# Induced attention and a PReLU layer in one kernel: casting weight loads, seven shared PSUM banks, weight folds ahead, idle matmuls, new planner constants

## The chip, the core and the metric

The kernel runs on one core of one Trainium2 chip. The metric is device time in microseconds (us), the median over several executions. The profiled span of an execution is some 2 us shorter than its device time. All profiles below are of single executions. An execution is called slow when it is over 1.5% above the fastest of the same kernel. In the profiles PE is TensorE (PEld its weight loads), DVE VectorE, ACT ScalarE, POOL GpSimd and SP SyncE. The granted clock is the share of TensorE's full clock that the profile records as allowed, 1.0 or 0.5 in these traces. A bank is one of the kernel's tiles in PSUM, the memory that its matmuls write to.

## The reference, cut to what matters

```python
# x: 4 x 12480 x 128 fp32, inducing: 32 x 128, w_in: 128 x 2048, w_out: 2048 x 128, alpha: 2048
def mab(q, kv):
    a = softmax(q @ kv.T / sqrt(128))
    return a @ kv
h = mab(inducing, x)            # per batch: 32 rows that sum up 12480
y = mab(x, h)                   # every row of x attends to the 32 rows of h
g = y @ w_in
out = (max(g, 0) + alpha * min(g, 0)) @ w_out
```

Since y is a weighted mean of 32 rows, the kernel folds h and both weight matrices into small matrices, once for each batch. It never forms the 2048-wide hidden layer, except in a fallback that this input does not need.

## The kernel before

Each of 4 batches has 9 chunks: 8 of 1536 rows and one of 192. A chunk goes through three stages, and each batch through one fold between the first and the second stage:

- A: load x as bf16 (POOL issues the casting load), flip it (DVE), scores (TensorE, 4 matmuls of 384 columns), exp (ACT), flip (DVE), sum into h (TensorE, 12 small matmuls).
- Fold: 20-odd dependent small steps from h to three small matrices SP, ZB, WB.
- S: second scores against h (TensorE), exp, and an extent for a later check.
- O: hidden (SP and mask matmuls), ReLU, ZB and WB matmuls into three banks, eviction with a scale (DVE, or ACT and then POOL), store of 768 KB.

A planner written in Python decides the order on every engine. It plays the tasks with assumed durations, takes the ready task of lowest deadline, and then emits the instructions in that order. The engines keep it whatever the chip does.

```python
RINGS = dict(xn=10, xt=16, s=3, h=1, o=4, e1=3, e1t=3, g=3, ob=4)   # s, h, o: PSUM banks
DR = "s"                                   # the folds' tiles come from the score banks
SLACK = 1.5                                # two numbers in the choice
BIAS = 0.2                                 # between DVE and ACT for evictions
OB = 0.35                                  # assumed time of the WB matmuls
TA, TS, TB, WL, LEAD = 2.6, 1.2, 3.2, 6, 2
def dl_a(b, i): return 2.0 * i if b == 0 else 18.0 + TA * (NCK * (b - 1) + i)   # stage A
def dl_w(b):    return dl_a(b, NCK) + WL
def dl_s(b, i): return dl_a(b, NCK) + TS if i <= 0 else dl_b(b, i) - LEAD        # stage S, fold
def dl_b(b, i): return dl_w(b) + TB * i                                          # stage O
# ... cut ...
def w_loads(_):                            # fp32, issued by SP as soon as it can
    nc.sync.dma_start(out=al[:], in_=moe_alpha.rearrange("(p k) -> p k", p=P))
    nc.sync.dma_start(out=w_in_f[:], in_=moe_w_in)
# ... w_out_f the same way; POOL then casts both to bf16 (1.9 us each) ...
```

The softmax here doesn't subtract the row's maximum and nothing guards it: scores larger than these inputs give would overflow.

## Time and profile before

| | before |
|---|---|
| device time | 177.68 us median of the first 3 runs (176.9 to 179.26) |
| first x landed / first scores | 10.8 / 13.8 us |
| fold of batch 0, from h copied to first hidden matmul | 28.8 to 46.5 us |
| first store issued | 50.8 us |
| end of the fold of batch 3 | 138.8 us |
| store interval in the tail | 3.1 us |

The page of the kernel before; rows of section 2 are 40 slices of 4.4 us, digits are tenths:

```profile
span 176.2 us, 3680 instructions
PE 134.5 (76%) x1322; PEld 65.4 (37%) x1322; DVE 117.4 (67%) x304; ACT 94.2 (53%) x279; POOL 77.6 (44%) x102
...
PEclk9999999659999969999999999997999995555555
DMA  4999999996899999999998586594398564787660
```

TensorE has most work, DMA is full for half of the span, and the granted clock is half over the last seven slices. The average does not show which of them counts; the stretches do. The timeline of the start (start, duration, engine, line, operation, tiles, count, and in brackets the idle time before it and what ended it):

```profile
1.21 0.41 SPq L832 DMA_DIRECT2D w_in_f<-in_moe_w_in_dram  x1
1.67 0.43 SPq L835 DMA_DIRECT2D w_out_f<-in_moe_w_out_dram  x1
1.30 2.83 POOL L357 DMA_DIRECT2D xn<-in_x_dram  x5 [0.35 <-issue]
10.85 0.98 DVE L364 STREAM_TRANSPOSE xt<-xn 128x768 f32<-128x768 f32 x1 [9.39 <-DMA xn<-in_x_dram]
13.83 1.46 PE L373 MATMUL s<-xt,blkI 128*128 128x384 bf16 x4 [13.83 <-ACT blkI L210]
```

One fp32 weight load leaves ahead of the first x load and one 0.4 us after it. They land at 6.3 and 11.0 us, and DVE waits 9.39 us for the first x. The timeline of batch 0's fold, its first and last links and one POOL cast:

```profile
28.84 0.26 ACT L435 COPY hp<-h 128x128 f32<-128x128 f32 x1
29.43 1.90 POOL L841 CAST w_in_b<-w_in_f 128x2048 bf16<-128x2048 f32 x1
```

```profile
46.47 0.24 PE L733 MATMUL hh<-e,sp 128*32 128x128 bf16 x3
```

Two windows of the tail (columns: window, length, busy time and count of PE, PEld, DVE, ACT, POOL, then granted clock, DMA share, GB/s), and one round of the circle in which it is caught, from the timeline:

```profile
140.00:150.00 10.00, 7.16 (x44) 2.45 (x42) 4.30 (x19) 4.97 (x14) 5.41 (x7) 0.73 0.49 170
150.00:160.00 10.00, 7.59 (x38) 2.00 (x37) 5.04 (x11) 2.84 (x7) 3.70 (x4) 0.50 0.86 310
```

```profile
153.21 1.01 PE L758 MATMUL o<-zb,e 128*128 128x512 bf16 x2 [0.93 <-DVE ob L779]
154.01 0.63 PE L758 MATMUL hh<-zb,e 128*128 128x512 bf16 x1
154.57 0.60 PE L767 MATMUL hh<-wb,g 32*128 32x512 bf16 x1
155.38 0.69 DVE L779 TENSOR_TENSOR ob<-hh,rd 128x512 f32<-128x512 f32 x1 [1.63 <-PE o L767]
156.13 1.01 PE L758 MATMUL o<-zb,e 128*128 128x512 bf16 x2 [0.55 <-DVE ob L779]
```

TensorE writes o, DVE evicts it, and the next ZB matmul waits 0.55 or 0.93 us for the bank. At half clock this takes 6.25 us for two chunks.

### The profile page before, as it was taken

How to read it: one execution, taken by the hardware profiler on the slowest of the kernel's cores; microseconds unless marked ns; L12 is line 12 of the kernel's file. 1: busy time of each engine (PE TensorE's matmuls, PEld its weight loads, DVE VectorE, ACT ScalarE, POOL GpSimd, SP SyncE). 2: the span in 40 equal slices, each digit the busy share in tenths (PEclk: the TensorE clock that was granted, in tenths of full speed). 3: DMA queues.
4: the chain of work that ended last, by engine and by line, in shares of the span. 5: the costliest groups of instructions: out<-in, count | busy, mean ns of one | idle time of the engine just before them, and what ended most of it. 6: DMA issues, size and time to landing. Idle time of an engine off the chain costs nothing.

```text
span 176.2 us, 3680 instructions
## 1 busy us (share of the span) xinstructions
PE 134.5 (76%) x1322; PEld 65.4 (37%) x1322; DVE 117.4 (67%) x304; ACT 94.2 (53%) x279; POOL 77.6 (44%) x102
## 2 busy tenths in 40 slices
PE   0006977699999888799998999978988967786600
PEld 0002433456554354355454555434435431121100
DVE  1059596779998997899799886781677553535300
ACT  2024434658377676547969874774875644222300
POOL 7510245409335423865422577332557446523220
PEclk9999999659999969999999999997999995555555
DMA  4999999996899999999998586594398564787660
GB/s 134 355 245 211 213 209 213 212 212 130 162 208 192 268 310 272 351 336 180 224 291 308 183 308 217 198 352 150 118 340 307 183 208 179 269 314 268 226 202 12
DMA packets 23433, 40.82 MB, mean 232 GB/s; under 512 B 1392, under 2 KB 19056, under 8 KB 23152
## 3 DMA queue, kind: packets, MB, share of 16 engines
q1 hardware_dynamic: 18160, 27.67, 44.1%
q0 software_dynamic: 5056, 12.78, 38.7%
q8 instruction: 12, 0.20, 0.4%
q10 hardware_dynamic: 192, 0.07, 0.2%
q14 instruction: 13, 0.11, 0.2%
HBM read 27.73 MB, written 25.56 MB: 303 GB/s over the span
## 4 chain that ended last, share of the span: by engine, by line
PE 54%; DVE 14%; DMA 14%; ACT 5%; issue 5%; POOL 2%; DVEq 0%; POOLq 0%; ACTq 0%
PE s L519 11%; PE s L373 11%; DMA out_dram<-ob 9%; PE o L758 8%; DMA xn<-in_x_dram 5%; DVE ob L779 5%; PE hh L767 5%; PE hh L758 4%; PE h L400 3%; ACT bh L210 3%; PE f L651 2%; PE hh L733 2%; PE hh L739 2%; POOL ob L795 2%; PE hwp L469 2%
## 5 line engine op out<-in xcount | busy, mean ns | idle before, releaser
L795 POOL TENSOR_TENSOR ob<-ob,rd 128x512 f32<-128x512 f32 (+1 forms) x44 | 44.6, 1027 | 45.4 <-ACT ob L784 38.6
L373 PE MATMUL s<-xt,blkI 128*128 128x384 bf16 (+1 forms) x144 | 30.9, 344 | 15.8 <-ACT blkI L210 13.8
L364 DVE STREAM_TRANSPOSE xt<-xn 128x768 f32<-128x768 f32 (+1 forms) x36 | 30.6, 864 | 9.5 <-DMA xn<-in_x_dram 9.4
L357 POOL DMA_DIRECT2D xn<-in_x_dram x36 | 19.9, 556 | 32.6 <-PE h L400 24.8
L519 PE MATMUL s<-xt,bh 128*128 128x384 bf16 (+1 forms) x144 | 30.3, 339 | 4.2 <-ACT bh L210 2.3
L758 PE MATMUL o<-zb,e 128*128 128x512 bf16 x64 | 23.7, 421 | 7.4 <-DVE ob L779 4.4
L779 DVE TENSOR_TENSOR ob<-hh,rd 128x512 f32<-128x512 f32 (+1 forms) x23 | 15.6, 676 | 17.2 <-PE o L767 11.5
L382 ACT ACTIVATE e<-s 128x384 bf16<-128x384 f32 (+1 forms) x36 | 16.6, 462 | 14.6 <-PE s L373 14.0
L784 ACT COPY ob<-o 128x512 f32<-128x512 f32 x31 | 18.1, 588 | 10.1 <-PE o L767 5.6
L373 PEld LDWEIGHTS <-blkI 128*128 128x128 bf16 (+1 forms) x144 | 13.1, 108 | 26.4 <-ACT blkI L210 13.8
L527 ACT ACTIVATE e<-s 128x384 bf16<-128x384 f32 (+1 forms) x36 | 16.6, 460 | 11.0 <-PE s L519 10.5
L779 DVE TENSOR_TENSOR ob<-o,rd 128x512 f32<-128x512 f32 x33 | 22.2, 677 | 0.0
L519 PEld LDWEIGHTS <-bh 128*128 128x128 bf16 (+1 forms) x144 | 12.8, 105 | 14.3 <-issue 3.5
L753 ACT ACTIVATE g<-hh 96x128 bf16<-96x128 f32 (+1 forms) x36 | 9.5, 266 | 14.8 <-DVE rd L745 12.8
L767 PE MATMUL hh<-wb,g 32*128 32x512 bf16 (+1 forms) x36 | 15.9, 441 | 0.0
L758 PE MATMUL hh<-zb,e 128*128 128x512 bf16 (+1 forms) x36 | 15.6, 433 | 0.1
L390 DVE STREAM_TRANSPOSE e1t<-e 128x192 f32<-128x192 f32 (+1 forms) x36 | 11.9, 343 | 3.9 <-ACT e L382 3.6
L767 PE MATMUL o<-wb,g 32*128 32x512 bf16 x64 | 14.2, 439 | 0.0
L758 PEld LDWEIGHTS <-e 128*128 128x128 bf16 (+1 forms) x100 | 9.4, 101 | 12.7 <-issue 9.1
L745 DVE RECIPROCAL rd<-hh 128x12 f32<-128x12 f32 (+1 forms) x36 | 7.7, 216 | 9.5 <-PE hh L739 9.5
L537 ACT ACTIVATE junk<-s 128x384 bf16<-128x384 f32 (+1 forms) x29 | 13.9, 480 | 0.0
L784 ACT COPY ob<-hh 128x512 f32<-128x512 f32 (+1 forms) x13 | 7.3, 558 | 8.4 <-PE o L767 2.8
(111 smaller groups left out, 168.8 us busy)
## 6 DMA issues: line engine op xcount, KB each, us to landing
out_dram<-ob SPq DMA_DIRECT2D x32, 768.0 KB, 4.0
xn<-in_x_dram POOLq DMA_DIRECT2D x32, 384.0 KB, 10.3
w_in_f<-in_moe_w_in_dram SPq DMA_DIRECT2D x1, 1024.0 KB, 5.1
w_out_f<-in_moe_w_out_dram SPq DMA_DIRECT2D x1, 1024.0 KB, 9.3
out_dram<-ob SPq DMA_DIRECT2D x4, 96.0 KB, 2.5
xn<-in_x_dram POOLq DMA_DIRECT2D x4, 48.0 KB, 9.5
ind<-in_inducing_dram ACTq DMA_DIRECT2D x4, 16.0 KB, 5.0
al<-in_moe_alpha_dram SPq DMA_DIRECT2D x1, 8.0 KB, 1.9
```

What stands on the lines that cost most here:

```text
L357: nc.gpsimd.dma_start(out=v["xn"][: c.p, : c.nk, :], in_=x[s.b, c.t0 : c.t0 + c.n, :].rearrange("(p j) c -> p j c", p=c.p),)
L364: nc.vector.transpose(out=xT[: c.p, : c.nk].rearrange("p k b j e -> p (k b j e)").bitcast(f32), in_=v["xn"][: c.p, : c.nk, :].bitcast(f32),)
L373: nc.tensor.matmul(v["sc"][: c.p, :], blkI[: c.p, bb, e, : c.na, :].rearrange("p a m -> p (a m)"), s.xT[c.i][: c.p, : c.nk, bb, :, e], sta ...
L382: nc.scalar.activation(out=v["e1"][: c.p, : c.w].rearrange("p (K j e) -> p K j e", j=M, e=2), in_=v["sc"][: c.p, :].rearrange("p (K e j) - ...
L519: nc.tensor.matmul(w["sc"][: c.p, :], BH[r][: c.p, bb, e, : c.na, :].rearrange("p a m -> p (a m)"), s.xT[c.i][: c.p, : c.nk, bb, :, e], st ...
L527: nc.scalar.activation(out=s.e2[: c.p, c.off : c.off + c.w].rearrange("p (r j k) -> p r j k", j=M, k=c.nkk), in_=w["sc"][: c.p, :].rearran ...
L537: nc.scalar.activation(out=junk[: c.p, : c.w], in_=w["sc"][: c.p, :], func=SQUARE, accum_out=amx[: c.p, 0, b, c.i : c.i + 1],)
L758: nc.tensor.matmul(o[: c.po, :], s.e2[: c.p, c.off + q * c.po : c.off + (q + 1) * c.po], ZB[r][: c.p].rearrange("p a c -> p (a c)"), start ...
L767: nc.tensor.matmul(v["o", q][: c.po, :], v["g"][rows, : c.po], WB[r][rows].rearrange("p a c -> p (a c)"), start=False, stop=True,)
L779: nc.vector.tensor_tensor(out=ob[: c.po, : c.na, q, :], in0=o[: c.po, : c.na, :], in1=bc(rd, [[1, c.na], [0, C]]), op=ALU.mult,)
L784: nc.scalar.copy(out=ob[: c.po, : c.na, q, :], in_=o[: c.po, : c.na, :])
L795: nc.gpsimd.tensor_tensor(out=ob, in0=ob, in1=bc(s.rd[: c.po, c.i, q, : c.na], [[1, c.na], [0, C]]), op=ALU.mult,)
```

## The change

Its intent: get the weights out of the way of the first x and save the casts on POOL; let any stage use any of seven PSUM banks, so that outputs can hold six; let the folds, on which all outputs of a batch wait, go first; keep TensorE's clock up with idle matmuls where the planner sees a pause. With it came new planner constants and four more buffers for flipped x (the room of the fp32 weights).

```diff
-RINGS = dict(xn=10, xt=16, s=3, h=1, o=4, e1=3, e1t=3, g=3, ob=4)
-DR = "s"
+RINGS = dict(xn=10, xt=20, p=7, h=1, e1=3, e1t=3, g=3, ob=4)
+CAPS = dict(A=3, S=3, F=7, O=6)          # stage A scores, stage S scores, folds, outputs
-SLACK = 1.5
-BIAS = 0.2
+SLACK = 3.0
+FILL = 0.5
+BIAS = 0.1
@@ Plan.play
+                if eng == "PE":
+                    self.fill(now, free.get(eng, 0.0))
+    def fill(self, now, end):
+        n = int(FILL * (now - end) / 0.22)
+        ok = [i for i, f in enumerate(self.free["p"]) if f is not None and f <= end]
+        if n > 0 and ok:                  # n matmuls of 512 columns on blkI, into a free bank
+            i = min(ok, key=lambda i: self.free["p"][i])
+            self.order.append(("PE", dict(fn=lambda _: self.filler(n), held={"p": (i, "")}, ...)))
@@ ... tasks take "p:A", "p:S", "p:F", "p:O" in place of "s" and "o" ...
-    OB = 0.35
-    TA, TS, TB, WL, LEAD = 2.6, 1.2, 3.2, 6, 2
+    PW = 16.5
+    FB = 100.0
+    OB = 0.42
+    TA, TS, TB, WL, LEAD = 2.2, 1.2, 3.5, 14, 1
@@ fold_batch
-        prio = dl_s(b, -1)
+        prio = dl_s(b, -1) - FB           # also for the first second scores and the later links
@@ weights
-        nc.sync.dma_start(out=w_in_f[:], in_=moe_w_in)
+        nc.gpsimd.dma_start(out=w_in_b[:], in_=moe_w_in)      # casts on the way, prio PW: after batch 0's x
@@ ... w_out the same; the two POOL casts are gone; the rest of the diff is cut ...
```

More of the change, by code (lines that the diff above doesn't have):

```diff
@@ L63, in __init__ @@
         self.tasks = []
-        self.rings = {k: dict(n=n, taken=0, back=[]) for k, n in RINGS.items()}
+        self.free = {k: [0.0] * n for k, n in RINGS.items()}
+        self.used = {}
+        self.now = None
+        self.before = None
     def add(self, eng, fn, deps=(), take=(), give=(), prio=0, bytes=0):
@@ L79, in play @@
         todo = list(self.tasks)
-        order = []
+        self.order = order = []
         while todo:
@@ L110, in play @@
                 for k in t["take"]:
-                    r = self.rings[k]
-                    i = r["taken"] - r["n"]
-                    if i >= 0:
-                        if r["back"][i] is None:
-                            blocked = True
-                            break
-                        at = max(at, r["back"][i] + self.HOP)
+                    k, c = (k + ":").split(":")[:2]
+                    f = min((f for f in self.free[k] if f is not None), default=None)
+                    if f is None or (c and self.used.get(c, 0) >= CAPS[c]):
+                        blocked = True
+                        break
+                    at = max(at, f + (self.HOP if f else 0.0))
                 if blocked:
@@ L134, in play @@
                 for k in t["take"]:
-                    r = self.rings[k]
-                    t["held"][k] = r["taken"]
-                    r["taken"] += 1
-                    r["back"].append(None)
+                    k, c = (k + ":").split(":")[:2]
+                    f = self.free[k]
+                    i = min((i for i in range(len(f)) if f[i] is not None), key=lambda i: f[i])
+                    f[i] = None
+                    t["held"][k] = (i, c)
+                    self.used[c] = self.used.get(c, 0) + 1
                 for k, owner in t["give"]:
-                    self.rings[k]["back"][owner["held"][k]] = end
+                    i, c = owner["held"][k]
+                    self.free[k][i] = end
+                    self.used[c] -= 1
                 todo.remove(t)
@@ L148, in play @@
         self.total = max(t["end"] for t in self.tasks)
-        self.order = order
+    def fill(self, now, end):
[3 more added lines that the diff above has]
+            i = min(ok, key=lambda i: self.free["p"][i])
+            self.order.append(("PE", dict(fn=lambda _: self.filler(n), held={"p": (i, "")}, start=end, end=end+n*.22, prio=0, eng={"PE":n*.22})))
     def emit(self):
         for eng, t in self.order:
+            self.now = t
             t["fn"](eng)
+        self.now = None
 @with_exitstack
@@ L196, with filler, make_slots, ring @@
     PS = bass.MemoryType.PSUM
-    pools = {}
-    for k, n in ((k, n) for k, n in RINGS.items() if n):
-        space = dict(space=PS) if k in ("s", "d", "h", "o") else {}
-        pools[k] = ctx.enter_context(tc.tile_pool(name="r_" + k, bufs=n, **space))
-    def ring(k, shape, dtype, name=None):
-        return pools[k].tile(shape, dtype, tag=k, name=name or k)
+    def filler(n):
+        p = ring("p")
+        for _ in range(n):
+            nc.tensor.matmul(
+                p[:], blkI[:, 0, 0].rearrange("p a m -> p (a m)"), blkI[:].rearrange("p b e a m -> p (b e a m)"),
+                start=True, stop=True,
+            )
+    plan = Plan()
+    plan.filler = filler
+    add = plan.add
+    slots, turn = {}, {}
+    def make_slots(shapes):
+        for k, (shape, dtype) in shapes.items():
+            pool = ctx.enter_context(
+                tc.tile_pool(name="r_" + k, bufs=1, **(dict(space=PS) if k in ("p", "h") else {}))
+            )
+            slots[k] = [pool.tile(shape, dtype, name=f"{k}{i}") for i in range(RINGS[k])]
+            turn[k] = 0
+    def ring(k, shape=None):
+        if plan.now:
+            i = plan.now["held"][k][0]
+        else:
+            i = turn[k]
+            turn[k] = (i + 1) % RINGS[k]
+            if k == "p":
+                turn[k] = max(2, turn[k])
+        t = slots[k][i]
+        if shape is None:
+            return t
+        n = math.prod(shape[1:])
+        t = t[: shape[0], :n]
+        return t if len(shape) == 2 else t.rearrange("p (a b) -> p a b", b=shape[2])
     def on(eng):
@@ L239 @@
     al = const.tile([P, KC], f32, name="al")
-    w_in_f = const.tile([C, DFF], f32, name="w_in_f")
-    w_out_f = const.tile([P, KC, C], f32, name="w_out_f")
     w_in_b = const.tile([C, DFF], bf16, name="w_in_b")
@@ L293, in small_act @@
             nc.scalar.copy(out=selq[rows, q], in_=sel4[rows])
+    make_slots(dict(
+        xn=([P, NK, C], bf16), xt=([P, NK, 2, M, 2], bf16), p=([P, 512], f32), h=([P, C], f32),
+        e1=([P, NK * M], bf16), e1t=([P, NK // 2, M, 2], bf16), g=([P, P], bf16),
+        ob=([P, G, NK // 4, C], f32),
+    ))
     flags = keep.tile([1, B + 1], i32, name="flags")
@@ L330, in dl_b @@
         return dl_w(b) + TB * i
-    plan = Plan()
-    add = plan.add
     def dve(n, fast=1):
@@ L343, in pool_batch @@
         s = bt[b]
-        s.xT, s.pr = [], []
+        s.xT = {}
         s.h = None
@@ L355, in load @@
         def load(_):
-            v["xn"] = ring("xn", [P, NK, C], bf16)
+            v["xn"] = ring("xn")
             nc.gpsimd.dma_start(
@@ L362, in flip @@
         def flip(_):
-            xT = ring("xt", [P, NK, 2, M, 2], bf16)
+            xT = ring("xt")
             nc.vector.transpose(
@@ L367, in flip @@
             )
-            s.xT.append(xT)
+            s.xT[c.i] = xT
         def scores(_):
-            v["sc"] = ring("s", [P, c.w], f32)
+            v["sc"] = ring("p", [P, c.w])
             for n, (bb, e) in enumerate(((0, 0), (0, 1), (1, 0), (1, 1))):
@@ L380, in exps @@
         def exps(_):
-            v["e1"] = ring("e1", [P, NK * M], bf16)
+            v["e1"] = ring("e1")
             nc.scalar.activation(
@@ L388, in flip_e @@
         def flip_e(_):
-            v["e1t"] = ring("e1t", [P, NK // 2, M, 2], bf16)
+            v["e1t"] = ring("e1t")
             nc.vector.transpose(
@@ L396, in sums @@
             if c.i == 0:
-                s.h = ring("h", [P, C], f32)
+                s.h = ring("h")
             for k in range(c.nk):
@@ L411, in pool_chunk @@
         s.flips.append(tf)
-        ts = add(("PE", 0.05 + 4 * c.w / 2400), scores, [tf], take=["s"], prio=prio)
-        te = add(("ACT", 0.23 + act(c.w)[1]), exps, [ts], take=["e1"], give=[("s", ts)], prio=prio)
+        ts = add(("PE", 0.05 + 4 * c.w / 2400), scores, [tf], take=["p:A"], prio=prio)
+        te = add(("ACT", 0.23 + act(c.w)[1]), exps, [ts], take=["e1"], give=[("p", ts)], prio=prio)
         tt = add(dve(c.w // 2), flip_e, [te], take=["e1t"], give=[("e1", te)], prio=prio)
@@ L431, in dtile @@
         def dtile(shape, name):
-            return ring(DR, shape, f32, name)
+            return ring("p", shape)
         def f_hp(_):
@@ L495, in fold_batch @@
         t = add(act(C), f_hp, [s.pooled], give=[("h", s.first_sum)], prio=prio)
-        t = t_tot = add(("PE", 0.35), f_tot, [t, small], take=[DR], prio=prio)
-        t_n = add(("DVE", 0.5), f_norm, [t], give=[(DR, t_tot)], prio=prio)
+        t = t_tot = add(("PE", 0.35), f_tot, [t, small], take=["p:F"], prio=prio)
+        t_n = add(("DVE", 0.5), f_norm, [t], give=[("p", t_tot)], prio=prio)
         t = add(("DVE", 0.22), f_flip, [t_n], prio=prio)
         t_b = [
-            add({"DVE": 0.28, "ACT": 0.3}, lambda e, a=a: blocks(a, e, BH[r], v["h4t"]), [t], prio=prio)
+            add({"DVE": 0.28, "ACT": 0.3}, lambda e, a=a: blocks(a, e, BH[r], v["h4t"]), [t] + s.free_h, prio=prio)
             for a in range(G)
         ]
-        t = t_hT = add(("PE", 0.15), f_hT, [t_n], take=[DR], prio=prio)
-        t = add(act(M), f_hTc, [t], give=[(DR, t_hT)], prio=prio)
-        t = t_hwp = add(("PE", 1.0), f_hwp, [t, w_in_done], take=[DR], prio=prio)
-        t_hw = add(act(KC * M), f_hw, [t], give=[(DR, t_hwp)], prio=prio)
+        t = t_hT = add(("PE", 0.15), f_hT, [t_n], take=["p:F"], prio=prio)
+        t = add(act(M), f_hTc, [t], give=[("p", t_hT)], prio=prio)
+        t = t_hwp = add(("PE", 1.0), f_hwp, [t, w_in_done], take=["p:F"], prio=prio)
+        t_hw = add(act(KC * M), f_hw, [t], give=[("p", t_hwp)], prio=prio)
         t = add(dve(KC * M), f_hs, [t_hw], prio=prio + 0.1)
@@ L516, in scores @@
             def scores(_):
-                w["sc"] = ring("s", [P, c.w], f32)
+                w["sc"] = ring("p", [P, c.w])
                 for n, (bb, e) in enumerate(((0, 0), (0, 1), (1, 0), (1, 1))):
@@ L547, in second @@
             ts = add(
-                ("PE", 0.05 + 4 * c.w / 2400), scores, t_b, take=["s"],
+                ("PE", 0.05 + 4 * c.w / 2400), scores, t_b, take=["p:S"],
                 give=[("xt", s.flips[c.i])], prio=pr,
@@ L554, in second @@
                 del either["DVE"]
-            tx = add(either, extent, [ts, te], give=[("s", ts)], prio=pr)
+            tx = add(either, extent, [ts, te], give=[("p", ts)], prio=pr)
+            s.scored.append(ts)
             return tx, te
-        s.extents, s.weighed = [], []
+        s.extents, s.weighed, s.scored = [], [], []
         for c in chunks:
-            tx, tq = second(c, dl_s(b, c.i))
+            tx, tq = second(c, dl_s(b, c.i) - (0.0 if c.i else FB))
             s.extents.append(tx)
             s.weighed.append(tq)
-        prio = dl_s(b, 0)
+        prio = dl_s(b, 0) - FB
         def g_ext(_):
@@ L690, in fold_batch @@
         t = add(("ACT", 0.3), g_ext, s.extents[:1], prio=prio)
-        t = t_dlp = add(("PE", 0.2), g_dlp, [t], take=[DR], prio=prio)
-        t = add(dve(M), g_dm, [t], give=[(DR, t_dlp)], prio=prio)
+        t = t_dlp = add(("PE", 0.2), g_dlp, [t], take=["p:F"], prio=prio)
+        t = add(dve(M), g_dm, [t], give=[("p", t_dlp)], prio=prio)
         t_st = add(("DVE", 0.7), g_st, [t, t_sg], prio=prio)
-        t = t_pos = add(("PE", 0.3), g_base, [t_st], take=[DR], prio=prio)
+        t = t_pos = add(("PE", 0.3), g_base, [t_st], take=["p:F"], prio=prio)
         t_sl = add(("DVE", 0.34), g_sl, [t_st], prio=prio)
@@ L697, in fold_batch @@
         t_p0 = add(dve(KC * CAP), g_pick, [t_pos], prio=prio)
-        t_fl = add(("DVE", 0.16), g_flag, [t_pos, t_p0], give=[(DR, t_pos)], prio=prio)
+        t_fl = s.flagged = add(("DVE", 0.16), g_flag, [t_pos, t_p0], give=[("p", t_pos)], prio=prio)
         t_om = add(("POOL", 1.05), g_om, [t_p0, t_sl], prio=prio)
-        t = t_fs = add(("PE", 1.0), g_fs, [t_p0], take=[DR], prio=prio)
-        t_s = add({"ACT": 0.22, "DVE": 0.18}, g_fzs, [t], give=[(DR, t_fs)], prio=prio)
-        t = t_f = add(("PE", 1.2), g_f, [t_om, t_p1, wo_done], take=[DR], prio=prio)
-        t = add({"ACT": 0.29, "DVE": 0.28}, g_fz, [t, t_s], give=[(DR, t_f)], prio=prio)
-        t = t_r = add(("PE", 0.3), g_rep, [t], take=[DR], prio=prio)
-        t = f1 = add(("DVE", 0.2), g_sp, [t, s.free_r], prio=prio)
-        f2 = add(dve(G * C), lambda _: g_blk(0, ZB[r], mask), [t, s.free_r], prio=prio)
-        f3 = add(dve(G * C), lambda _: g_blk(1, WB[r], afmask), [t, f2, s.free_r],
-                 give=[(DR, t_r)], prio=prio)
+        t = t_fs = add(("PE", 1.0), g_fs, [t_p0], take=["p:F"], prio=prio)
+        t_s = add({"ACT": 0.22, "DVE": 0.18}, g_fzs, [t], give=[("p", t_fs)], prio=prio)
+        t = t_f = add(("PE", 1.2), g_f, [t_om, t_p1, wo_done], take=["p:F"], prio=prio)
+        t = add({"ACT": 0.29, "DVE": 0.28}, g_fz, [t, t_s], give=[("p", t_f)], prio=prio)
+        t = t_r = add(("PE", 0.3), g_rep, [t], take=["p:F"], prio=prio)
+        t = f1 = add(("DVE", 0.2), g_sp, [t] + s.free_r, prio=prio)
+        f2 = add(dve(G * C), lambda _: g_blk(0, ZB[r], mask), [t] + s.free_r, prio=prio)
+        f3 = add(dve(G * C), lambda _: g_blk(1, WB[r], afmask), [t, f2] + s.free_r,
+                 give=[("p", t_r)], prio=prio)
         s.folded = [f1, f2, f3]
@@ L721, in emit_batch, with one @@
         r = b % 2
-        def one(c):
+        def one(c, before):
             prio = dl_b(b, c.i)
@@ L729, in hidden @@
             def hidden(_):
-                v["hh"] = hh = ring("o", [P, 512], f32, "hh")
+                v["hh"] = hh = ring("p")
                 for q in range(c.nq):
@@ L750, in relu @@
             def relu(_):
-                v["g"] = ring("g", [P, P], bf16)
+                v["g"] = ring("g")
                 rows = slice(0, c.nq * M)
@@ L755, in outs_a @@
             def outs_a(q):
-                v["o", q] = o = v["hh"] if q == 0 else ring("o", [P, G * C], f32)
+                v["o", q] = o = v["hh"] if q == 0 else ring("p")
                 nc.tensor.matmul(
@@ L773, in move @@
                 if q == 0:
-                    v["ob"] = ring("ob", [P, G, NK // 4, C], f32)
+                    v["ob"] = ring("ob")
                 rd = s.rd[: c.po, c.i, q, : c.na]
@@ L800, in one @@
             th = add(
-                ("PE", 0.15 + 0.02 * c.nq), hidden, [s.weighed[c.i]] + s.folded, take=["o"], prio=prio,
+                ("PE", 0.2 + 0.02 * c.nq), hidden, [s.weighed[c.i], before] + s.folded, take=["p:O"], prio=prio,
             )
@@ L807, in one @@
             for q in range(1, c.nq):
-                tos.append(add(("PE", 0.22), lambda _, q=q: outs_a(q), [th], take=["o"], prio=prio))
+                tos.append(add(("PE", 0.22), lambda _, q=q: outs_a(q), [th], take=["p:O"], prio=prio))
             to = add(("PE", 0.22), lambda _: outs_a(0), [tr, ti] + tos, prio=prio)
@@ L813, in one @@
                     {"DVE": 0.675, "ACT": 0.57, "ACT4": 1.5}, lambda e, q=q: move(e, q),
-                    [t_ob] + moves[:1], take=["ob"] if q == 0 else [], give=[("o", tos[q])], prio=prio,
+                    [t_ob] + moves[:1], take=["ob"] if q == 0 else [], give=[("p", tos[q])], prio=prio,
                 )
@@ L823, in one, with al_load, w_in_load @@
             add(("NONE", 0.0), lambda _: None, [td], give=[("ob", moves[0])], prio=prio)
-            return th, t_ob
-        last = [one(c) for c in chunks][-1]
-        s.emitted = last
-    def w_loads(_):
+            return th, t_ob, tos[-1]
+        s.formed = []
+        for c in chunks:
+            s.emitted = one(c, plan.before)
+            s.formed.append(s.emitted[1])
+            plan.before = s.emitted[2]
+    def al_load(_):
         nc.sync.dma_start(out=al[:], in_=moe_alpha.rearrange("(p k) -> p k", p=P))
-        nc.sync.dma_start(out=w_in_f[:], in_=moe_w_in)
+    def w_in_load(_):
+        nc.gpsimd.dma_start(out=w_in_b[:], in_=moe_w_in)
     def w_out_load(_):
-        nc.sync.dma_start(out=w_out_f[:], in_=moe_w_out.rearrange("(p k) c -> p k c", p=P))
+        nc.gpsimd.dma_start(out=WO[:], in_=moe_w_out.rearrange("(p k) c -> p k c", p=P))
     def weights():
-        tw = add(("SP", 0.2), w_loads, [bt[0].loads[2]], prio=17, bytes=2 ** 20)
-        tw2 = add(("SP", 0.1), w_out_load, [bt[0].loads[5]], prio=17.5, bytes=2 ** 20)
-        w_in_done = add(
-            ("POOL", 1.95), lambda _: nc.gpsimd.tensor_copy(out=w_in_b[:], in_=w_in_f[:]), [tw], prio=18
-        )
+        ta = add(("SP", 0.1), al_load, prio=0, bytes=2 ** 13)
+        w_in_done = add(("POOL", 0.6), w_in_load, prio=PW, bytes=2 ** 20)
+        wo_done = add(("POOL", 0.6), w_out_load, prio=PW + 0.1, bytes=2 ** 20)
         om_done = add(
@@ L847, in weights @@
             ),
-            [tw], prio=18.1,
+            [ta], prio=18.1,
         )
-        t = add(
-            ("POOL", 1.95), lambda _: nc.gpsimd.tensor_copy(out=WO[:], in_=w_out_f[:]), [tw2], prio=24
-        )
-        wo_done = t
         return w_in_done, om_done, wo_done
@@ L867 @@
         s.first_sum = next(t for t in plan.tasks[n0:] if "h" in t["take"])
-        s.free_r = bt[b - 2].emitted[1] if b >= 2 else None
-        s.free_h = bt[b - 2].emitted[0] if b >= 2 else None
+        s.free_r = bt[b - 2].formed if b >= 2 else []
+        s.free_h = bt[b - 2].scored if b >= 2 else []
         fold_batch(b)
@@ L883, in check @@
         )
-        tp = ring(DR, [P, B, M], f32, "tp")
+        tp = ring("p", [P, B, M])
         nc.tensor.matmul(tp[:], ones_f[:], tops[:], start=True, stop=True)
@@ L896, in check @@
         nc.vector.tensor_copy(out=flags[:], in_=flags_f[:])
-    tck = add(("DVE", 2.5), check, [t for s in bt for t in s.extents], take=[DR], prio=dl_b(B - 1, NCK))
-    add(("NONE", 0.0), lambda _: None, [tck], give=[(DR, tck)], prio=dl_b(B - 1, NCK))
+    tck = add(
+        ("DVE", 2.5), check, [t for s in bt for t in s.extents + [s.flagged]], take=["p:F"], prio=dl_b(B - 1, NCK),
+    )
+    add(("NONE", 0.0), lambda _: None, [tck], give=[("p", tck)], prio=dl_b(B - 1, NCK))
     with tc.manual_schedule():
@@ L911, in factors @@
         nc.vector.tensor_tensor(
-            out=W1[:], in0=w_out_f[:], in1=bc(om[:], [[1, KC], [0, C]]), op=ALU.mult
+            out=W1[:], in0=WO[:], in1=bc(om[:], [[1, KC], [0, C]]), op=ALU.mult
         )
@@ L919, in whole @@
         for j in range(DFF // 512):
-            hp = ring("s", [P, 512], f32, "hkp")
+            hp = ring("p")
             for q in range(G):
@@ L930, in whole @@
         )
-        zp = ring("s", [P, C], f32, "zp")
+        zp = ring("p", [P, C])
         for k in range(KC):
@@ L940, in whole @@
         for c in chunks:
-            ob = ring("ob", [P, G, NK // 4, C], f32, "obw")
+            ob = ring("ob")
             for a in range(c.na):
                 rows = slice(a * M, (a + 1) * M)
-                acc = ring("o", [P, NK // 4, C], f32, "acc")
+                acc = slots["p"][a % 2][:, : NK // 4 * C].rearrange("p (a b) -> p a b", b=C)
                 for q in range(c.nq):
@@ L951, in whole @@
                 for f in range(KC):
-                    ph = ring("s", [P, c.w], f32, "ph")
+                    ph = ring("p", [P, c.w])
                     nc.tensor.matmul(
```

## The prediction

> **What bounds the kernel now.** Four stretches of the 176.2 us have four limits.
>
> 1. Start, 0 to 14 us. The chain of waits opens with 9.53 us of "DMA xn<-in_x_dram". The timeline shows why: both fp32 weight loads (2 MB) are issued at 1.2 and 1.7 us and land at 6.3 and 11.0; the first x lands at 10.8. First matmul: 13.8 us.
> 2. 10 to 42 us. DMA share in the windows view is 1.08 at 212 GB/s (bf16 side): one x chunk every 1.86 us. TensorE pauses.
> 3. Fold of batch 0. From copying h (28.8 us) to the first hidden matmul (46.5) is 17.7 us; the first store is issued at 50.8. Between the links stand scores of other chunks, two POOL weight casts of 1.9 us, and a halved clock (0.66 in the 30 to 40 us window).
> 4. 50 to 140 us: TensorE 80 to 100% busy, DVE mostly 71 to 92% (windows view); DMA is full until 90 us, 0.5 to 0.85 after. Tail, 142 to 165 us: clock 0.55, a repeating circle of ZB matmuls 1.0, WB 0.6, eviction 0.7, bank freed; two chunks take 6.25 us. The four "o" banks and the clock set it, not DMA (0.69).
>
> **Costs.**
> - Weights behind the first x: I expect the first x at about 5.5 us (the quickest load took 4.6), first scores near 8.5. This saves about 5 us of head, as batch 0 is paced by its loads. The DMA work stays: 1 MB of bf16 at 211 GB/s is 5 us, later, against some 6.5 before. The POOL casts (3.8 us) vanish.
> - Folds ahead: the links of one fold, added up from the timeline, are about 12 us against 17.7; I expect first stores 4 us earlier. Later folds are overlapped; little comes of them.
> - Seven shared banks, six for outputs: in the tail a second chunk can start while the first is evicted. With the clock held, 1.0 and 0.6 become 0.6 and 0.39. Then 768 KB at about 360 GB/s (moved bytes over busy share) sets 2.15 us per chunk against 3.1: 6 to 7 us over seven chunks.
> - Idle matmuls: they hold the clock in the tail and at 32 to 38 us; two 3.4 us cold spells in the middle vanish. The Trainium skill, "TensorE: Matmul & The Clock Gate", Part 1, says a window of about 3.4 us without enough work halves the clock; this trace agrees (o<-wb matmuls 0.39 us warm, 0.60 after 144.6 us). Cost: they run in order, so real work arriving earlier than planned waits. I subtract 2 us.
> - The middle stays bound by TensorE and DVE (117 us busy): perhaps 2 us gained.
>
> **Floors** (estimates from these rates): x 61 + weights 5 + stores 71 = 137 us of DMA; TensorE about 111 us if warm and dense.
>
> Sum: 176 - 5 - 4 - 6.5 - 2 + 2 = about 161 profiled; on the clock of the runs **162 us, 80% range 154 to 171**. Faster by over 2%: 0.93; within 2%: 0.05; slower: 0.02.
>
> **Right if** the first x lands by 6 us; the first store is issued near 41 us; the granted clock stays near 1.0 to the end; the tail takes under 2.5 us per chunk at DMA share 0.9; DVE share rises to 72% or more.
>
> **Wrong if** fillers delay real matmuls in the full middle; the fold still takes 17 us; shared banks bind stages together; the weights delay batch 0's fold (they must land by 24 us).

## The result, and the profile after

| | before | after |
|---|---|---|
| device time, same rounds | 178.38 us median of 4 | 168.06 us median of 4 (167.86 to 172.95, the last one slow) |
| first x landed / first scores | 10.8 / 13.8 us | 6.1 / 13.7 us |
| fold of batch 0 | 28.8 to 46.5 us | 26.4 to 44.3 us |
| first store issued | 50.8 us | 50.3 us |
| end of the fold of batch 3 | 138.8 us | 127.4 us |
| last store issued | 168.4 us | 159.1 us |
| mean store interval, 27th to 35th | 3.0 us | 2.1 us |

The ratio is 0.9425, with a 95% interval of 0.9333 to 0.9517. A ratio is the mean time of one kernel's fast runs over that of the other's of the same rounds, so not quite the ratio of the medians quoted. The page after:

```profile
span 166.1 us, 3746 instructions
PE 134.3 (81%) x1344; PEld 67.4 (41%) x1353; DVE 117.6 (71%) x304; ACT 91.6 (55%) x276; POOL 79.0 (48%) x106
...
PEclk9999999699999969999999999995978999999555
DMA  4999999999899999999996698762459699989951
```

TensorE's busy time did not change (134.5 and 134.3 us), although the second has idle matmuls in it. The clock's cold end is shorter, and DMA is full again near the end. The start, from the timeline after:

```profile
6.13 0.98 DVE L413 STREAM_TRANSPOSE xt<-xn 128x768 f32<-128x768 f32 x1 [4.66 <-DMA xn<-in_x_dram]
7.61 1.52 ACT L257 COPY blkI<-ind_t 32x128 bf16<-32x128 bf16 x2 [3.72 <-DVE ind_t L281]
9.19 4.69 PE L218 MATMUL p<-blkI 128*128 128x512 bf16 x11 [9.19 <-ACT blkI L257]
13.71 0.82 PE L422 MATMUL p<-xt,blkI 128*128 128x384 bf16 x4
```

The first x came 4.7 us earlier. But at 9.19 us, when the block matrix blkI was ready and the first scores could have started, 11 idle matmuls started in their place. They read blkI, so they could not start sooner, in the pause for which they were planned. They took 4.69 us at half speed (0.43 us from start to start, against 0.22 for those at 14.4 us), and the scores began at 13.71 us: 0.12 us earlier than before. Batch 0's fold, from the timeline after:

```profile
26.43 0.27 ACT L484 COPY hp<-h 128x128 f32<-128x128 f32 x1 [0.60 <-PE h L449]
```

```profile
31.34 2.72 PE L568 MATMUL p<-xt,bh 128*128 128x384 bf16 x8
32.04 0.32 ACT L617 ACTIVATE dsel<-sel,amx 128x32 f32<-128x32 f32 x1
33.86 0.39 PE L621 MATMUL p<-dsel,ones_f 128*128 128x32 f32 x2
34.75 2.12 PE L568 MATMUL p<-xt,bh 128*128 128x384 bf16 x12
41.37 2.12 PE L422 MATMUL p<-xt,blkI 128*128 128x384 bf16 x12
41.57 0.19 DVE L729 TENSOR_TENSOR sp<-p,mask 128x32 bf16<-128x32 f32 x1
44.26 0.22 PE L783 MATMUL p<-e,sp 128*32 128x128 bf16 x3
```

From h copied to the first hidden matmul it is 17.8 us, against 17.6 (46.47 less 28.84) before. "Ahead" is only the planner's rank: when a link is not yet ready by the plan, other scores go into TensorE's queue, here 8, 12 and 12 matmuls, and the next link stands behind them. The link dsel is written by 32.36 us and its matmul starts at 33.86; SP is written by 41.76 us and the first hidden matmul starts at 44.26. The tail after, in the same windows as before, and some lines of its timeline:

```profile
140.00:150.00 10.00, 9.02 (x72) 3.55 (x69) 6.33 (x15) 5.12 (x16) 5.28 (x6) 1.00 0.92 325
150.00:160.00 10.00, 4.83 (x27) 1.75 (x25) 4.85 (x18) 3.67 (x12) 4.07 (x4) 0.68 0.84 293
```

```profile
142.53 0.81 PE L568 MATMUL p<-xt,bh 128*128 128x384 bf16 x4
145.53 0.82 PE L568 MATMUL p<-xt,bh 128*128 128x384 bf16 x4
149.21 0.83 PE L568 MATMUL p<-xt,bh 128*128 128x384 bf16 x4
150.51 0.36 PE L568 MATMUL p<-xt,bh 96*96 96x64 bf16 x4
153.56 0.80 PE L935 MATMUL p<-tops,ones_f 128*128 128x128 f32 x2 [1.63 <-DVE tops L930]
```

The clock is 1.00 up to 153.5 us, and DMA moves 325 GB/s where it moved 170. No idle matmul holds this clock: all 28 in the trace start between 9.2 and 28 us. What stands between the output chunks is second scores of batch 3 (p<-xt,bh), up to 150.9 us. In the kernel before these ended at 140.1 us, and the clock fell at 144.6:

```profile
139.81 0.33 PE L519 MATMUL s<-xt,bh 96*96 96x64 bf16 x4
```

The stores say where the gain lies. Up to the 26th of 36, issued at 140.5 us before and 138.0 after, the two kernels are within 3 us for most stores, and for some the change is behind. The last ten bring the other 7 us: from the 27th to the 35th the mean interval is 3.0 us before and 2.1 us after.

### The profile page after: what moved, and what is told of

The parts are those of the page before. It is cut to its first block, busy times and chain, and to the rows that moved or that the text cites. A ratio compares the mean times of both kernels' runs of the same rounds, so it can differ in the third digit from the quotient of the medians.

```text
span 166.1 us, 3746 instructions
## 1 busy us (share of the span) xinstructions
PE 134.3 (81%) x1344; PEld 67.4 (41%) x1353; DVE 117.6 (71%) x304; ACT 91.6 (55%) x276; POOL 79.0 (48%) x106
## 5 line engine op out<-in xcount | busy, mean ns | idle before, releaser
L829 DVE TENSOR_TENSOR ob<-p,rd 128x512 f32<-128x512 f32 (+1 forms) x52 | 33.1, 674 | 8.8 <-PE p L817 6.0
L808 PE MATMUL p<-zb,e 128*128 128x512 bf16 (+1 forms) x94 | 33.0, 398 | 3.2 <-ACT g L803 1.5
L834 ACT COPY ob<-p 128x512 f32<-128x512 f32 (+1 forms) x48 | 26.0, 582 | 10.5 <-PE p L817 7.1
L568 PE MATMUL p<-xt,bh 128*128 128x384 bf16 (+1 forms) x144 | 27.9, 330 | 3.4 <-DVE bh L259 1.6
L422 PE MATMUL p<-xt,blkI 128*128 128x384 bf16 (+1 forms) x144 | 27.2, 312 | 0.1
L431 ACT ACTIVATE e<-p 128x384 bf16<-128x384 f32 (+1 forms) x36 | 16.7, 464 | 17.1 <-PE p L422 16.6
L576 ACT ACTIVATE e<-p 128x384 bf16<-128x384 f32 (+1 forms) x36 | 16.6, 464 | 13.7 <-PE p L568 13.5
L218 PE MATMUL p<-blkI 128*128 128x512 bf16 x28 | 10.0, 473 | 9.5 <-ACT blkI L257 9.2
L422 PEld LDWEIGHTS <-blkI 128*128 128x128 bf16 (+1 forms) x144 | 12.7, 102 | 10.0 <-issue 1.7
L817 PE MATMUL p<-wb,g 32*128 32x512 bf16 (+1 forms) x100 | 15.0, 407 | 0.1
L449 PE MATMUL h<-xn,e1t 128*32 128x128 bf16 x392 | 11.8, 228 | 0.8 <-DVE e1t L439 0.6
L586 ACT ACTIVATE junk<-p 128x384 bf16<-128x384 f32 (+1 forms) x26 | 12.2, 469 | 0.0
```

The lines of the kernel that those rows point to most:

```text
L422: nc.tensor.matmul(v["sc"][: c.p, :], blkI[: c.p, bb, e, : c.na, :].rearrange("p a m -> p (a m)"), s.xT[c.i][: c.p, : c.nk, bb, :, e], sta ...
L431: nc.scalar.activation(out=v["e1"][: c.p, : c.w].rearrange("p (K j e) -> p K j e", j=M, e=2), in_=v["sc"][: c.p, :].rearrange("p (K e j) - ...
L449: nc.tensor.matmul(s.h[q * M : (q + 1) * M, :], v["e1t"][: c.p, k // 2, :, k % 2], v["xn"][: c.p, k, :], start=(c.i == 0 and k < G), stop= ...
L568: nc.tensor.matmul(w["sc"][: c.p, :], BH[r][: c.p, bb, e, : c.na, :].rearrange("p a m -> p (a m)"), s.xT[c.i][: c.p, : c.nk, bb, :, e], st ...
L576: nc.scalar.activation(out=s.e2[: c.p, c.off : c.off + c.w].rearrange("p (r j k) -> p r j k", j=M, k=c.nkk), in_=w["sc"][: c.p, :].rearran ...
L808: nc.tensor.matmul(o[: c.po, :], s.e2[: c.p, c.off + q * c.po : c.off + (q + 1) * c.po], ZB[r][: c.p].rearrange("p a c -> p (a c)"), start ...
```

## The experiments

Twelve kernels ran besides the change, all with right results. The medians are of all runs of a kernel, slow ones too (three of four in a_nofill and a_xt16, three of six in n1, two of five in b_weights, one of four in the change, a_fb0 and b_fold); the ratios are of fast runs, against the kernel before of the same rounds. In "order kept" runs no engine's order of other work differs from the kernel they are made from; idle matmuls do not enter the planner's times, so taking them away keeps the order. Where a planner input was changed the whole order shifts, and luck of a few us is possible.

| run | median us | ratio (95%) | what |
|---|---|---|---|
| the change | 168.06 | 0.9425 (0.9333 to 0.9517) | |
| a_nofill | 167.26 | none (one fast run, 163.51) | no idle matmuls; order kept |
| a_nolead | 164.49 | 0.9226 (0.9163 to 0.9289) | first burst of idle matmuls gone; order kept |
| a_split | 170.36 | 0.9551 (0.9480 to 0.9622) | banks 3 + 4 |
| a_split_nofill | 170.98 | 0.9552 (0.9464 to 0.9640) | the same, no idle matmuls; order kept |
| a_fb0 | 175.82 | 0.9838 (0.9753 to 0.9924) | folds not ahead |
| a_oldc | 173.26 | 0.9697 (0.9625 to 0.9769) | old constants |
| a_xt16 | 172.56 | none (one fast run, 167.96) | 16 flipped-x buffers |
| b_weights | 183.92 | 1.0280 (1.0206 to 1.0354) | before + the weights' part |
| b_w_order | 179.49 | 1.0048 (0.9973 to 1.0123) | the same, order kept |
| b_fold | 191.17 | 1.0644 (1.0535 to 1.0753) | before + folds ahead |
| n1 | 166.99 | 0.9273 (0.9183 to 0.9363) | a_nolead + 4 constants |
| n2 | 170.04 | 0.9498 (0.9410 to 0.9587) | n1 + folds ahead by 2 only |

### The idle matmuls

```diff
 a_nofill, from the change:
-FILL = 0.5
+FILL = 0.0
 a_nolead, from the change:
-        n = int(FILL * (now - end) / 0.22)
+        n = int(FILL * (now - end) / 0.22) if end else 0     # none before the first real matmul
```

Expected of a_nofill:

> The changed kernel with no idle matmuls at all; the order of all other instructions stays the same, as fillers do not enter the plan's times. In the changed kernel all 28 traced idle matmuls start between 9.2 and 28 us, 11 of them in one burst of 4.7 us right before the first scores. Theory H (the burst delays the first scores and eats the head's gain; the gain of the whole change comes from the banks in the tail): first scores near 9.2 us instead of 13.7, but cold ones (1.46 us per chunk); time 165 to 169 us. Rival F (the fillers' warm clock is a main source of the gain): 172 us or more.

Expected of a_nolead:

> The changed kernel without the first burst of 11 idle matmuls alone; later ones stay. Theory H: first scores near 9.2 us, fold of batch 0 begins 2 to 4 us earlier than 26.4 us, and up to that much of it reaches the end: 164 to 167 us. If the middle is bound by engines whatever the start, the end moves by less than 1 us: 167 to 168. Rival F (the burst pays by warming the clock): slower than 168.

Measured: a_nolead 164.49 us, the only interval clear below that of the change. Its first scores, from its timeline:

```profile
9.13 1.46 PE L422 MATMUL p<-xt,blkI 128*128 128x384 bf16 x4 [9.13 <-ACT blkI L257]
10.39 1.91 PE L218 MATMUL p<-blkI 128*128 128x512 bf16 x4
```

They start 4.6 us earlier, cold (1.46 us for four where the change has 0.82), and the next four idle matmuls follow them, where DVE has to flip the second chunk. The fold of batch 0 begins at 23.3 us instead of 26.4. Up to the 21st store the lead is 1.6 to 2.0 us; it is 2.8 at the 22nd and 4.9 at the last store but one (the 35th, issued at 152.3 us instead of 157.2). The growth sets in just after a cold spell that the change has at 122.8 us and this trace has not; whether the burst brings that spell about was not tested. So theory H held for the first scores and the time, and the rival that the burst pays by warming the clock fell: the burst costs 3.6 us of medians, of which the head start itself is about half. The other half of theory H, that the gain comes from the banks, is tested next. In a_nofill three of four runs were slow (167.2 to 167.4 us at a granted clock of 0.897) and one was fast (163.51 us at 0.928, below theory H's range). Against fast runs of a_nolead (164.1 to 165.7) the remaining idle matmuls bring nothing; that they make slow runs rarer (0 of 4 against 3 of 4) is suggested by these counts, not shown.

### The banks

```diff
 a_split, from the change (a_split_nofill: also FILL = 0.0):
-CAPS = dict(A=3, S=3, F=7, O=6)
+CAPS = dict(A=3, S=3, F=3, O=4)
-                    if f is None or (c and self.used.get(c, 0) >= CAPS[c]):
+                    if f is None or (c and self.used.get(c, 0) >= CAPS[c]) or (
+                        c and c != "O" and sum(self.used.get(u, 0) for u in "ASF") >= 3):
```

Expected of a_split:

> The changed kernel with the seven banks split as before: at most 3 for scores and folds together, at most 4 for outputs; everything else stays. Theory S (the six output banks make the tail): the last stores come 3 us apart instead of 2, and most of the 10 us is lost: 174 to 179 us. Rival O (order and constants alone bring the last fold 11 us earlier and fill the tail): 167 to 170 us.

Measured: 170.36 us, 2.3 us over the change, with intervals that overlap a little. Theory S fell; O was right to within half a microsecond. With four output banks the stores of the tail come 1.8 us apart (27th to 35th), not 3. Its trace has what the change lacks, 15 idle matmuls after 130 us.

Expected of a_split_nofill:

> The run with the banks split three and four, and no idle matmuls as well. The split run took 170.4 us; its trace has idle matmuls between the output chunks of the tail, and the clock stays at 1.0 there until 159 us, where the kernel before has 0.5 from 144.6 us on. Theory C (with four output banks the idle matmuls keep the clock, and with it the tail's pace): tail at clock 0.5 and near 3 us per chunk as in the kernel before; the 3.6 us of the first burst come back, but the tail loses 6 to 8 us: 172 to 176 us. Rival (the tail's pace is set by order, not by the clock): 166 to 168 us, the 3.6 us of the burst gained and nothing lost.

Measured: 170.98 us. Windows of a_split and then of a_split_nofill:

```profile
140.00:150.00 10.00, 9.52 (x75) 3.35 (x73) 7.76 (x18) 4.49 (x12) 5.17 (x5) 1.00 0.94 333
```

```profile
140.00:150.00 10.00, 9.74 (x49) 2.25 (x47) 5.59 (x13) 3.23 (x9) 3.77 (x4) 0.50 0.87 306
```

Without idle matmuls the clock is 0.50 here (from 132.2 to 152.7 us in all), with them 1.00, and DMA moves 306 against 333 GB/s. At the 25th store a_split_nofill is still 0.9 us ahead (138.8 against 139.7 us), the remainder of what it saved at the start; at the 35th it is 2.6 us behind (160.5 against 157.9). So idle matmuls do what they are for where the planner puts them into a tail: 3.5 us between these two traces. Theory C had the mechanism right and the size too large: 170.98 us lies between the two ranges. Even with a cold clock the stores came 2.6 us apart (22nd to 32nd), not 3.

### The folds' priority

```diff
 a_fb0, from the change:
-    FB = 100.0
+    FB = 0.0
 b_fold, from the kernel before:
-        prio = dl_s(b, -1)
+        prio = dl_s(b, -1) - 100.0
-            tx, tq = second(c, dl_s(b, c.i))
+            tx, tq = second(c, dl_s(b, c.i) - (0.0 if c.i else 100.0))
-        prio = dl_s(b, 0)
+        prio = dl_s(b, 0) - 100.0
```

Expected of a_fb0:

> The changed kernel with the folds at their old priority; all else stays. Theory P (folds ahead bring the last fold's end to 127 us from 139 us and so start the tail early): last fold's end at 132 us or later, 171 to 176 us. Rival (the folds' priority changes little, since each fold waits in TensorE's queue behind scores either way: 17.8 us against 17.7 for batch 0): 166 to 170 us.

Measured: 175.82 us. Theory P held. The fold of batch 3 in a_fb0 and then in the change (its first link, h copied, and the writing of SP near its end):

```profile
113.49 0.29 ACT L484 COPY hp<-h 128x128 f32<-128x128 f32 x1
136.34 0.19 DVE L729 TENSOR_TENSOR sp<-p,mask 128x32 bf16<-128x32 f32 x1 [0.60 <-PE p L723]
```

```profile
107.36 0.26 ACT L484 COPY hp<-h 128x128 f32<-128x128 f32 x1
125.99 0.19 DVE L729 TENSOR_TENSOR sp<-p,mask 128x32 bf16<-128x32 f32 x1 [1.15 <-PE p L723]
```

It starts 6.1 us later and takes 22.9 us instead of 18.6. For batch 0 the same pair is 26.6 to 42.7 us against 26.4 to 41.6, only some 1 us. So the part that I had called small, the later folds, is where the priority pays.

Expected of b_fold:

> The kernel before with only the folds' priority moved ahead of all other work, constants and banks old. Undoing this in the changed kernel cost 7.8 us. Theory P (folds ahead gain by themselves): last fold ends before 134 us, 171 to 175 us. Rival I (they pay only together with the retuned deadlines and the shared banks, because a fold that goes first starves the stores): 178 us or more.

Measured: 191.17 us; theory P fell here, rival I held. By itself the same priority costs 12.7 us. Two windows of b_fold around its second fold:

```profile
60.00:70.00 10.00, 9.28 (x77) 5.21 (x77) 7.23 (x19) 5.40 (x18) 3.38 (x5) 0.66 1.07 323
70.00:80.00 10.00, 9.41 (x137) 5.21 (x136) 8.98 (x23) 6.41 (x20) 8.36 (x10) 1.00 0.56 166
```

Between the fourth store (61.0 us) and the fifth (74.5 us) none is issued, and in the second window the DMA share is down to 0.56. The same priority stands in a_split (old split of the banks, 170.36 us) and in a_oldc (old constants, 173.26 us), both faster than the kernel before. So neither of the two alone makes it lose once the rest of the change is there. Why it loses where both are old was not taken apart further.

### The planner's constants and the buffers of flipped x

```diff
 a_oldc, from the change:
-SLACK = 3.0        -BIAS = 0.1        -OB = 0.42
+SLACK = 1.5        +BIAS = 0.2        +OB = 0.35
-    TA, TS, TB, WL, LEAD = 2.2, 1.2, 3.5, 14, 1
+    TA, TS, TB, WL, LEAD = 2.6, 1.2, 3.2, 6, 2
 a_xt16, from the change:
-RINGS = dict(xn=10, xt=20, p=7, ...)
+RINGS = dict(xn=10, xt=16, p=7, ...)
```

Expected of a_oldc:

> The changed kernel with the planner's old constants (deadlines of the stages, assumed cost of the output matmuls, the two that choose an engine for evictions); banks, folds, weights, idle matmuls stay. Theory O (the retuned order makes most of the gain): 173 to 179 us. Rival S2 (banks, folds and weights make it): 166 to 170 us.

Expected of a_xt16:

> The changed kernel with 16 instead of 20 buffers for flipped x (the four extra ones are what the dropped fp32 weights paid for). Theory X (these let batch 3's loads run ahead: the last x lands at 85.6 us against 93 us before): last x at 90 us or later, 170 to 174 us. Rival: 167 to 169 us.

Measured: a_oldc 173.26 us, so theory O held at the low end of its range; the constants are worth 5.2 us, half of the gain rather than most of it. Its last x lands at 97.2 us instead of 85.6, and the fold of batch 3 ends at 141.5 us. a_xt16 is inconclusive: three of four runs were slow, the fast one took 167.96 us, as the change does, and in its profile (of a slow run) the last x landed at 83.2 us, so nothing speaks for theory X.

### The weights alone

```diff
 b_weights, from the kernel before: the weights' part of the diff, with PW = 16.5
 b_w_order, from the kernel before, planner untouched:
             # in the load of x
+            if s.b == 0 and c.i == NCK - 1:
+                nc.gpsimd.dma_start(out=w_in_b[:], in_=moe_w_in)
+                nc.gpsimd.dma_start(out=WO[:], in_=moe_w_out.rearrange("(p k) c -> p k c", p=P))
             # SP's loads of w_in and w_out and POOL's two casts become empty tasks
```

Expected of b_weights:

> The kernel before with only the weights changed: casting loads behind the first batch's x, POOL casts gone. My prediction's term: 5 us less, 172 to 174 us, with the first scores near 9.2 us and the first store near 46 us. Rival M (the middle and the tail are bound by engines and banks, so a head start is lost there): first scores 4.5 us earlier, but the end within 2 us of before, 176 to 179 us.

Measured: 183.92 us, slower than both theories allowed. In its profile, which is of a slow run, first scores came at 9.4 us and the first store at 47.9, as hoped; but the planner, told of other loads, chose another order, in which the last x lands at 98.1 us and the fold of batch 3 ends at 147.6.

Expected of b_w_order:

> The kernel before with the weights as casting loads issued right after batch 0's last x, POOL casts gone, and every engine's order of all other work kept exactly as before (the run with the planner free to reorder took 183.9 us). Theory R (the loss of that run came from the new order that the planner chose; the loads themselves give a head start that passes to the end, as the run without the first burst showed): first scores near 9.3 us, 173 to 176 us. Rival L (the later weights and batch 1's later x cost as much as the head gives): 177 us or more.

Measured: 179.49 us, the same as before (1.0048); theory R fell and rival L held. Its timeline shows where 4.5 us of lead went:

```profile
22.71 0.36 PE L374 MATMUL s<-xt,blkI 96*96 96x64 bf16 x4
28.05 1.46 PE L374 MATMUL s<-xt,blkI 128*128 128x384 bf16 x4 [4.97 <-DVE xt L365]
29.44 0.61 PE L401 MATMUL h<-xn,e1t 128*32 128x128 bf16 x14
```

In the old order the first scores of batch 1 stand ahead of the last 14 sums of batch 0. With the weights between the two batches, batch 1's first x lands at about 27 us, and TensorE waits 4.97 us with batch 0's sums behind it. Batch 0's fold starts at 30.1 us, later than the 28.8 of the kernel before. The Trainium skill, "TensorE: Matmul & The Clock Gate", Part 3, says that matmuls keep strict program order; this wait agrees. In the change the last sums of batch 0 (25.98 us) run before the first scores of batch 1 (34.09 us), so there the fold's start does not queue behind batch 1.

### Towards a better version

```diff
 n1, from a_nolead:                       n2, from n1:
-TA = 2.2  WL = 14  LEAD = 1    BIAS = 0.1    -FB = 100.0  SLACK = 3.0  TB = 3.5
+TA = 2.0  WL = 10  LEAD = 1.5  BIAS = 0.2    +FB = 2.0    SLACK = 3.5  TB = 3.3
```

Expected of n1:

> A version meant to beat both: the changed kernel without the first burst of idle matmuls, and four planner constants moved (scores of later batches planned closer, outputs 4 us earlier, second scores half a step earlier, evictions leaning less to VectorE); folds at the full new priority. If the plan's order carries to the chip as it did for the other runs, 160 to 163.5 us; if the gain of a plan of this size is lost in the clock's cold spells, 164 to 166 us.

Expected of n2:

> As the run before, but folds ahead by 2 us of deadline only instead of 100, with slightly closer output deadlines. If absolute priority of the folds is what brings the gain, this is slower than it by 3 us or more: 165 us or more. If a mild priority is enough once deadlines fit, 160 to 164 us, and the stores' gap during the last fold (110 to 115 us in the changed kernel, DMA share 0.14) is smaller.

Measured: n1 has three fast runs at 165.4 to 166.0 us and three slow ones up to 172.2, so its fast runs lie in the second of its two ranges; n2 has 170.04 us. Neither beats a_nolead. n2 is 4.4 us slower than n1 by medians of fast runs (165.6), so the first of its two cases held, with the caution that two more constants differ. The best kernel is a_nolead, the change less the first burst, at 164.49 us.

## Why the prediction was right or wrong

The time (162, range 154 to 171) held 168.06 us, and "faster" was right. The gain was forecast as 15.7 us from 177.68 and came to 10.3. That it fell inside the range is in part luck: the 9 us forecast for the head and batch 0's fold moved the first store by less than 1 us, and 5.2 us come from constants that were not in the sum. Term by term:

- Weights behind the first x, "saves about 5 us of head": the first x landed at 6.1 us (forecast 5.5, and "by 6"), but the first scores moved by 0.12 us. The failed link was the cost that I gave the idle matmuls: I subtracted 2 us for delays in the middle, and did not see that the first pause, from zero to the first scores, would be filled too, by work that depends on the same blkI. a_nolead shows this burst at 3.6 us. b_w_order shows a second condition that I missed: the lead is lost if the next batch's x stands ahead of the fold.
- Folds ahead, "first stores 4 us earlier; later folds are overlapped; little comes of them": wrong in both halves. Batch 0's fold kept its 17.8 us, for the links queue behind other scores on TensorE, so the sum of the links (12 us) was no estimate; the first store was issued at 50.3 us, not near 41. The priority is worth 7.8 us when it is taken from the change (a_fb0), and batch 0's fold moved by only some 1 us of that.
- Six banks and the clock, "6 to 7 us" in the tail: the size of the tail's gain was about right (7 us over the last ten stores), its causes were not. Four output banks cost 2.3 us, at the edge of what these rounds resolve. The clock did stay up in the tail, but no idle matmul ran there. The traces show second scores spread into the tail instead, and the half clock beginning 2.6 us after the last of them in the change and 4.5 us after in the kernel before. That spreading them is the cause is read from these traces; no run moved them alone. A rival is untested: the last nine stores come 2.2 us apart in the change and 1.8 to 2.3 in all nine runs made from it, but 3.0 in the kernel before and 2.8 to 3.0 in the three made from it. So no part that was taken away singly brings the old pace back. The cut rest of the diff lets a task take whichever bank is free, where before they came in turn, and makes each output chunk wait in the plan for the ZB matmuls of the chunk before; no run took these two away.
- "Two 3.4 us cold spells in the middle vanish": they did not; the clock was 0.5 at 30.6, 57.9, 112.5 and 122.8 us, 3.4 us each.
- The constants were not in my sum at all. Undoing them costs 5.2 us (a_oldc).
- "Under 2.5 us per chunk at DMA share 0.9" in the tail: right (0.92; 2.1 us). "DVE share rises to 72% or more": just missed (71%).

The removals do not add up: folds 7.8, constants 5.2, banks 2.3 make 15.3 us where the whole is 10.3, and folds or weights alone make the kernel before slower. The parts are worth what the order makes of them.

## What to carry to other kernels

A filler must depend on nothing that the real work waits for; otherwise it starts when the real work could start and pushes it back by its own length. In a kernel with a fixed order per engine, cost a part of a change by the order it leads to, not by its links: look at what stands in front of the moved work in the in-order queue. And test a part both ways, taken from the new kernel and added to the old one: the folds' priority gains 7.8 us in the one and loses 12.7 in the other.

## What the Trainium skill lacked or had wrong

- "TensorE: Matmul & The Clock Gate", the table of advice near its end, asks for no idle gaps over some 3 us between bursts. That is not enough: in the kernel before the clock fell at 144.6 us after 3.4 us in which TensorE was busy for 2.1, and it stayed at 0.5 to the end of the matmuls near 166 us, all with no gap over 0.94 us. Part 1 of the page does tell of short idle times between groups of matmuls that made a kernel's clock swing. Which busy share suffices the page does not say, and no run here settles it: of the two windows from 140 to 150 us shown above, the one of a_split_nofill has 9.74 us of 10 busy at a clock of 0.50, the one of a_split 9.52 at 1.00.
- The same page, Part 1, gives N / 1.2 GHz, 426.7 ns at N = 512, from start to start of cold matmuls. This agrees: the 11 idle matmuls of 512 columns start 0.427 us apart, but for one step of 0.40. The page also says that whatever is issued in the first 3.4 us or so runs cold. What it does not warn of is that matmuls meant to warm the clock, queued in front of ready work, push that work back: by 4.6 us here (9.13 to 13.71 us).
- Nothing is wrong with "DMA: Bandwidth & Descriptors" here, but the figure has to be chosen. Its Specifications give about 358 GB/s as the limit of memory per core, by halving what two cores share; only one ran here. The casting loads of x went beyond it: 212 GB/s on the bf16 side from 10 to 30 us of the change, so by our estimate twice that, 424 GB/s, of fp32 read. That agrees with the 425 GB/s that its section "Bandwidth" measured for a large load by one core alone. Stores stayed near the first figure, 353 GB/s at a share of 0.99 from 130 to 140 us of the change.
